# A two-layer mixture-of-experts kernel: first tiles by columns, one unit's gathers in a row, half blocks interleaved with whole ones

## The chip, the cores and the metric

The kernel runs on one core of a Trainium2 chip. The metric is the device time of one execution in microseconds (us): the median of three runs of the kernel before is 1027.73 us, the lowest 1024.75 and the highest 1029.03. TensorE (PE) multiplies matrices, VectorE (DVE), ScalarE (ACT) and GpSimd (POOL) do the rest, and SyncE (SP) and POOL issue most transfers.

## The reference

```python
x = windowed_attention(q, k, v, mem_k, mem_v)   # 4 x 8 heads x 768 x 64 -> 3072 tokens x 512
# layer 1: every token goes to one expert, each expert holds at most 3072 / 8 = 384 tokens
for e in range(8):
    mask = assigned == e                         # greedy, by falling logit
    out[mask] = np.maximum(x[mask] @ w1[e], 0) @ w2[e]      # 512 -> 1024 -> 512
x = out
# layer 2: every token goes to its two best experts by noisy logits, weighted by their softmax
for e in range(8):
    for k in range(2):
        mask = top2[:, k] == e
        out[mask] += top2_w[mask, k, None] * (np.maximum(x[mask] @ w1[e], 0) @ w2[e])
```

## The kernel before

After the attention (about the first tenth of the time) and the routing of the first expert come the eight experts of layer 1, one after the other, and then the eight of layer 2. An expert's tokens are fetched by indirect DMAs of POOL (gathers of 128 tokens into `xg`), transposed into `xT`, multiplied with the first weights into 8 tiles of the hidden layer (`mm1`, 12 matmuls each: 4 pieces of the 512 inputs, and 3 products of the high and low fp16 parts `w_jh`, `w_jl`), put through the relu, and multiplied with the second weights (`mm2`: 24 matmuls of 512 columns for each block of 128 tokens). The results of layer 2 (`z`, `pv`) are scattered into the output by POOL.

In layer 1 an expert has three blocks of 128 tokens. For k = 0 and k = 1 the gathered tokens are transposed by PE (8 transposes of 128x128 each into a PSUM tile `tps`, copied to `xT` by ACT), for later ones by a transposing DMA of SP.

In layer 2 an expert e has two units, numbered u = 2e and u = 2e + 1. The first holds blocks 0, 1 and 2 and, for e = 0 to 5, a half block (HALF = 3): 64 tokens for e = 0, 1, 2 (2 parts) and 32 for e = 3, 4, 5 (4 parts). The second holds blocks 4, 5 and 6. A half block is computed in 24 steps; a step splits the 512 output columns over its parts, so that 2 matmuls of 64x256 (4 of 32x128) stand side by side in PE's columns, on 64 (32) columns of weights each.

One main program issues PE's matmuls. Between them it calls `tick()`, which runs generators for all that lies beside: gathers, transposes, weight splits, routing, lists. A generator yields a planned time or a condition; a planner's cost of each instruction (`Pipe.account`) decides between which matmuls it is resumed. All instructions recorded so have line L68. Where the main program waits (`until`, `wait` with a `spare` tile), it issues matmuls on `ones` as filling. Every engine works its instructions off in the order in which they were issued. PSUM tiles come from pools: m1 has three buffers (tiles of `mm1`), m2 two (tiles of `mm2`, and `tps` before).

What the change touches: `split` (the weights' scaling), `mm1`, `mm2`, `transpose`, `gather1` (layer 1's gathers), `list2` (token lists of layer 2; a small matmul `dup` copies a half block's list, `lsh`, to the other partitions), `gathers2` (layer 2's gathers and transposes), `metas` (small DVE work on gathered tokens) and `moe1`, `moe2` (the main program). SP issues, in one queue, the transposing DMAs (`xT<-xg`) and the loads of the next weights (`st<-x_dram`).

Of the kernel before, what the change touches and what calls it, by code (L numbers as in the profile page):

```python
# [29 lines left out]
CAP = NTOK // E  # L30
# [1044 lines left out]
C_H = 1.0  # L1075

KF = 5
SLACKG = -200.0

METAS = 16000.0  # L1080
LATE = 6000.0
SLACKH = 500.0


def whole(i):
# [57 lines left out]
def split(ctx, i, st, eager):  # L1143
# [59 lines left out]
    def halves(j, s):  # L1203
        done = W["w1" if m == 0 else "w2"]
        n = order(i, j)
        yield lambda: ctx.wnext == n < len(ctx.wfree)
        ctx.wnext += 1
        hi, lo = (wp.tile([128, 1024], F16, tag=f"w{o}", name=f"w{i}_{j}{o}", bufs=12) for o in "hl")
        src = st[j]
        sj = s[:, j : j + 1]  # L1210
        yield max(pipe.t["s"] - 100, pipe.rdy("s", s))
# [24 lines left out]
    for j in range(4):  # L1236
        if i == 0 and j > 1:
            yield lambda: 0 in ctx.X1
# [30 lines left out]
    return ctx.m1.tile([128, DM], F32, tag="m1", name="m1")  # L1269


def mm1(ctx, k, xT, n, ps, last=True):

    pipe, W, hT = ctx.pipe, ctx.W[k], []
    for ft in range(FT):
        if ft:

            pipe.until(lambda: len(hT) > ft - 3)
            ps = tile1(ctx)
        if ft % 2 == 0:  # L1280
# [3 lines left out]
        ps = ps[:, :n]  # L1284
        fs = slice(128 * (ft % 2), 128 * (ft % 2) + 128)
        i = 0
        for kt in range(KT):
            for wo, xo in ((0, 0), (0, 1), (1, 0)):
                pipe.P.matmul(
                    ps, w1[wo][:, kt, fs], xT[:, KT * xo + kt, :n], start=(i == 0), stop=(i == 3 * KT - 1)  # L1290
                )
                i += 1
                if i < 3 * KT:
                    pipe.tick()
        h = ctx.hp.tile([128, 2, XN], F16, tag="hT", name="hT", bufs=FT + 1)
        if k < KF:
            h = h.rearrange("p o n -> p (o n)").bitcast(F32)[:, :n]
# [41 lines left out]
    return ps  # L1339


def mm2_f32(ctx, k, hT):

    pipe = ctx.pipe
# [13 lines left out]
    return ps  # L1358


def transpose(ctx, xT, rows, tile_):

    pipe = ctx.pipe
    yield pipe.rdy("p", tile_)
    ps = ctx.m2.tile([128, 2 * KT, 128], F16, tag="m2", name="tps")
    for kt in range(2 * KT):
        pipe.P.transpose(ps[:, kt], rows[:, 128 * kt : 128 * kt + 128], ctx.id16)
    pipe.S.activation(xT, ps, AF.Copy)


def gather1(ctx, k):

    pipe = ctx.pipe
    NA = CAP // 128
    xT = ctx.xp.tile([128, 2 * KT, XN], F16, tag="xT", name=f"xT{k}", bufs=3)
    ix = ctx.wk.tile([128, NA], F32, tag="ix1", name=f"ix1_{k}")
    xg = []
    yield pipe.rdy("g", ctx.idx1)
# [13 lines left out]
    for a in range(NA):  # L1392
        rows = xg[a][:, :DM].bitcast(F16)
        if k > 1:
            yield pipe.rdy("y", xg[a])
            pipe.D.dma_start_transpose(xT[:, :, 128 * a : 128 * a + 128], rows)
        else:
            yield from transpose(ctx, xT[:, :, 128 * a : 128 * a + 128], rows, xg[a])
# [120 lines left out]
def moe1(ctx):  # L1519
# [37 lines left out]
        pipe.add(g)  # L1557

    for k in range(E):
        ps = tile1(ctx)  # L1560
        if not k:
            pipe.until(lambda: 0 in ctx.gathered)
        pipe.until(lambda: k in ctx.X1 and k in ctx.W, ps)
        xT, ix = ctx.X1[k]
        hT = mm1(ctx, k, xT, CAP, ps)
        m1_done.add(k)
        ys = ctx.wk.tile([128, NA], F32, tag="ys", name=f"ys{k}")
        if k >= KF:
# [13 lines left out]
def list2(ctx, e, pi, wt, cols, late=0.0):  # L1582
# [12 lines left out]
    if HALF in cols:  # L1595
        h, m = cols.index(HALF), 128 // parts(e)
        sh = pool.tile([64, 3], F16, tag="lsh", name=f"lsh{e}")[:m]
        V_.tensor_copy(sh, six[:m, h])
        yield pipe.rdy("p", sh)
        pd = ctx.ms.tile([128, 3], F32, tag="mso", name=f"dup{e}")  # L1600
        P_.matmul(pd, ctx.dup[parts(e)][:m], sh, start=True, stop=True)
        V_.tensor_copy(six[:, h], pd)
# [88 lines left out]
def gathers2(ctx):  # L1691
    pipe, wk = ctx.pipe, ctx.wk
    V_ = pipe.V
    for e in range(E):
        for h, cols in enumerate(units(e)):
# [5 lines left out]
            xg = []  # L1701
            for a in cols:
                rows = ctx.rows2[e, a][0]
                yield max(pipe.rdy("g", rows), pipe.t["g"] - 100)
                g = ctx.xp.tile([128, ROW], F32, tag="xg", name=f"xg2_{e}_{a}", bufs=4)
                pipe.G.indirect_dma_start(
                    out=g, out_offset=None, in_=x2[:, :], in_offset=bass.IndirectOffsetOnAxis(ap=rows, axis=0)
# [2 lines left out]
            for a, g in zip(cols, xg):  # L1710
                m = 128 // parts(e) if a == HALF else 128
                s0 = 128 * (a - a0)
                yield pipe.rdy("y", g)
                pipe.D.dma_start_transpose(xT[:, :, s0 : s0 + m], g[:m, :DM].bitcast(F16))
            ctx.X2[u] = xT
# [4 lines left out]
def metas(ctx, e, u, cols, xg, meta):  # L1720
# [1 line left out]
    pipe, wk = ctx.pipe, ctx.wk  # L1722
    V_ = pipe.V
    na, a0 = len(cols), cols[0]
    yield pipe.rdy("v", *xg) + METAS * min(1.0, 0.5 * u)
    for a, g in zip(cols, xg):
        V_.tensor_copy(meta[:, a - a0], g[:, DM : DM + 2])
    tg = wk.tile([128, na], I32, tag="tg2", name=f"tg2_{u}", bufs=4)
# [40 lines left out]
def moe2(ctx):  # L1769
    pipe = ctx.pipe  # L1770
    for e in range(E):
        k = E + e
        for h, cols in enumerate(units(e)):
# [6 lines left out]
            ys = ctx.wk.tile([128, len(cols)], F32, tag="ys2", name=f"ys2_{u}")  # L1780
            pipe.V.tensor_scalar(ys, xw, ctx.W[k]["comb"], 1.0 / (C_H * WSC), op0=ALU.mult, op1=ALU.mult)
            pv = ctx.pv.pop(u, None)
            for c, a in enumerate(cols):
                ps = mm2(ctx, k, hT, 128 * c, parts(e) if a == HALF else 1, a == NA2 - 1)
                n = DM // parts(e) if a == HALF else DM
                if e:
                    z = pv[c]
# [130 lines left out]
def program(tc, t):  # L1918
# [3 lines left out]
    with (  # L1922
# [6 lines left out]
        with tc.manual_schedule(), tc.tile_pool(name="rt", bufs=1) as ctx.rt:  # L1929
            setup(ctx, cp)  # L1930
            attention(ctx)
            with (
# [12 lines left out]
                ctx.pipe.early.add(ctx.x2.tensor.name)  # L1945
                ctx.closed, ctx.sure, ctx.listed, ctx.est_known, ctx.gathered, ctx.spread = {}, {}, set(), set(), set(), 0
                ctx.st, ctx.split, ctx.W, ctx.wfree = {}, {}, {}, [0.0] * 12
                ctx.X1, ctx.Y, ctx.rowed, ctx.picked, ctx.gated = {}, {}, set(), 0, 0
                ctx.rows2, ctx.X2, ctx.M, ctx.pv, ctx.got2, ctx.u_done = {}, {}, {}, {}, set(), set()
                ctx.ovready = ctx.locked = ctx.ordered = False  # L1950
# [151 lines left out]
```

## Time and profile before

| | |
|---|---|
| median of three runs | 1027.73 us |
| profiled execution: device time | 1033.36 us |
| profiled execution: span | 1031.5 us |
| mean granted clock of PE | 0.983 |
| PE busy | 982.5 us, 95% of the span |
| DVE, ACT, POOL busy | 62%, 45%, 28% |

The span runs from the first instruction to the last; the device time is 1.9 us longer. PE is busy nearly all the time, so the order of PE's instructions is the order of the whole: time is gained where PE stands idle, or where it has less to do. What PE waited for is grouped in the view of waits; starts of single matmuls are in the timeline. The ends of matmuls are modelled, so the distance from one start to the next is the measure of what one takes.

### The profile page before, as it was taken

The page shows a single profiled execution, that of the slowest core. Times are in us where ns is not written, and L with a number is a line of the kernel's source. Part 1 is how long each engine was busy: PE and PEld are TensorE (multiplying, and loading weights), DVE is VectorE, ACT ScalarE, POOL GpSimd, SP SyncE. Part 2 cuts the span into 40 slices and gives each one's busy share as a digit, 9 for nine tenths or more (in the row PEclk, how much of TensorE's full clock was granted, in tenths as well). Part 3 has the DMA queues.
Part 4 walks back from the last instruction along what each step waited for, and adds up shares of the span by engine and source line. Part 5 has one row for each costly group of instructions (what it writes and reads, how often), then busy time and mean ns, then how long its engine had stood idle before and what let it go on. Part 6 is the DMA issues. An engine that isn't in the chain of part 4 may idle for free. (4 is left out here: it accounts for less than half of the span.)

```text
span 1031.5 us, 21798 instructions
## 1 busy us (share of the span) xinstructions
PE 982.5 (95%) x8278; PEld 589.7 (57%) x8278; DVE 639.0 (62%) x2095; ACT 466.7 (45%) x799; POOL 284.4 (28%) x468
## 2 busy tenths in 40 slices
PE   8989399999999999999989899999999999999997
PEld 5778377676767674554454454555544555555553
DVE  7988875676586776886757745457355454654221
ACT  6767153545262557977136445054260441523110
POOL 4765051010120312030223133133332332232221
PEclk9999599999999999999999999999999999999999
DMA  9998345575776759596188739367284591554410
GB/s 333 330 324 305 112 173 185 125 220 170 217 201 216 137 177 303 169 241 126 48 239 249 183 93 300 72 182 205 76 265 107 142 264 59 170 121 103 122 62 31
DMA packets 146848, 184.61 MB, mean 179 GB/s; under 512 B 105154, under 2 KB 105666, under 8 KB 145204
## 3 DMA queue, kind: packets, MB, share of 16 engines
q1 hardware_dynamic: 129410, 131.73, 44.7%
q0 software_dynamic: 13872, 45.15, 15.1%
q10 hardware_dynamic: 3458, 6.30, 1.7%
q8 instruction: 66, 1.08, 0.4%
q14 instruction: 42, 0.34, 0.1%
HBM read 127.10 MB, written 32.44 MB: 155 GB/s over the span
## 5 line engine op out<-in xcount | busy, mean ns | idle before, releaser
L68 PEld LDWEIGHTS <-hT 128*128 128x128 f16 (+2 forms) x1800 | 143.4, 98 | 163.3 <-issue 7.8
L68 ACT ACTIVATE hT<-m 128x384 f16<-128x384 f32 (+2 forms) x152 | 75.4, 499 | 282.2 <-PE m L68 258.3
L68 DVE SCALAR_TENSOR_TENSOR hT<-m,hT 128x384 f16<-128x384 f32 (+2 forms) x152 | 86.5, 570 | 105.6 <-ACT hT L68 91.2
L68 ACT ACTIVATE junk<-st 128x1024 f16<-128x1024 f32 x108 | 113.6, 1052 | 58.2 <-DMA st<-w_dram 30.2
L68 PE MATMUL m2f<-st,hT 128*128 128x256 f32 x480 | 127.6, 398 | 0.3 <-ACT hT L68 0.3
L68 POOL DMA_INDIRECT out_dram<-pv,ts x47 | 49.6, 1055 | 262.7 <-DVE pv L68 101.9
L68 DVE SCALAR_TENSOR_TENSOR pv<-m,ys,pv 128x512 f32<-128x512 f32 (+2 forms) x47 | 33.5, 714 | 117.4 <-PE m L68 117.3
L68 PE MATMUL m<-xT,w_0h 128*128 128x384 f16 (+2 forms) x384 | 97.9, 335 | 4.7 <-DMA xT<-xg 4.7
L68 PE MATMUL m<-xT,w_2h 128*128 128x384 f16 (+2 forms) x384 | 97.2, 333 | 1.7 <-DVE hT L68 1.7
L68 PE MATMUL m<-xT,w_3h 128*128 128x384 f16 (+2 forms) x384 | 97.1, 333 | 1.0 <-DVE hT L68 1.0
L68 PE MATMUL m<-xT,w_1h 128*128 128x384 f16 (+2 forms) x384 | 96.5, 331 | 0.0
L68 PEld LDWEIGHTS m2f<-st,hT 128*128 128x128 f32 x480 | 83.3, 190 | 10.0 <-ACT hT L68 0.7
L68 PE MATMUL m<-w_3h,hT 128*128 128x512 f16 (+2 forms) x300 | 71.7, 345 | 1.4 <-DVE hT L68 1.4
L68 PE MATMUL m<-w_2h,hT 128*128 128x512 f16 (+2 forms) x300 | 72.0, 345 | 0.9 <-issue 0.9
L68 PE MATMUL m<-w_0h,hT 128*128 128x512 f16 (+2 forms) x300 | 72.1, 346 | 0.0
L68 PE MATMUL m<-w_1h,hT 128*128 128x512 f16 (+2 forms) x300 | 71.5, 345 | 0.0
L68 PE MATMUL m<-xT,w_0l 128*128 128x384 f16 (+2 forms) x192 | 64.2, 335 | 0.0
L68 PE MATMUL m<-xT,w_2l 128*128 128x384 f16 (+2 forms) x192 | 64.0, 333 | 0.0
L68 PE MATMUL m<-xT,w_3l 128*128 128x384 f16 (+2 forms) x192 | 63.8, 332 | 0.0
L68 PE MATMUL m<-xT,w_1l 128*128 128x384 f16 (+2 forms) x192 | 63.5, 331 | 0.0
L68 POOL DMA_INDIRECT xg<-x,rows x54 | 54.2, 1004 | 29.5 <-issue 14.5
L68 POOL DMA_INDIRECT pv<-out_dram,tg x47 | 46.0, 979 | 51.7 <-DMA out_dram<-pv,ts 35.0
(350 smaller groups left out, 1827.4 us busy)
## 6 DMA issues: line engine op xcount, KB each, us to landing
st<-w_dram SPq DMA_DIRECT2D x64, 512.0 KB
st<-x_dram SPq DMA_DIRECT2D x64, 512.0 KB
v<-vctx_dram SPq DMA_DIRECT2D x24, 520.0 KB
k<-kT_dram SPq DMA_DIRECT2D x24, 312.0 KB
xr<-rb SPq DMA_DIRECT2D x24, 264.0 KB
x<-rb SPq DMA_DIRECT2D x24, 264.0 KB
q<-qT_dram SPq DMA_DIRECT2D x12, 512.0 KB
out_dram<-zero ACTq DMA_DIRECT2D x24, 256.0 KB
```

The lines of the kernel that those rows point to most:

```text
L68: return f(*args, **kw)
```

## The change

1. First expert (k = 0): a new function `first` computes the first two tiles of `mm1` by blocks of 128 columns, each as soon as its block of `xT` is copied, in 72 matmuls of 128 columns instead of 24 of 384. `xT` of k = 0 is stored block by block. Two of the weight splits wait for `X1` at another place.
2. Second expert (k = 1): its PE transposes are planned 3000 ns later (2 FAR1).
3. The matmul `dup` is planned 1500 ns later (FAR1).
4. Second unit of layer 2's first expert (u = 1): the gathers of blocks 4, 5 and 6 follow in a row, and block 6 is transposed by PE into an m1 buffer in place of a DMA. The eight transposes stand in PE's order inside unit 0's blocks 2 and HALF, behind the 16th matmul of block 2.
5. `metas` of unit 0 is planned 8000 ns later.
6. `mm2_both`: block 2 of a first unit and its half block are computed together. Nine matmuls of the whole block come first; then each further one is followed by one or two steps of the half block in turn.

```diff
+def first(ctx, tiles, spare):
+    pipe, W = ctx.pipe, ctx.W[0]
+    pipe.until(lambda: len(W["w1"]) > 0, spare)
+    w1 = W["w1"][0]
+    for a in range(CAP // 128):
+        pipe.until(lambda: len(ctx.part0) > a and ctx.part0[a][1] <= pipe.t["p"] + 60.0, spare)
+        pipe.wait(*w1, spare=spare)
+        xT = ctx.part0[a][0]
+        for ft, ps in enumerate(tiles):
+            i = 0
+            for kt in range(KT):
+                for wo, xo in ((0, 0), (0, 1), (1, 0)):
+                    pipe.P.matmul(
+                        ps[:, 128 * a : 128 * a + 128], w1[wo][:, kt, 128 * ft : 128 * ft + 128], xT[:, KT * xo + kt],
+                        start=(i == 0), stop=(i == 3 * KT - 1),
+                    )
...
+def mm2_both(ctx, k, hT, s0, s1, cut):
+    pipe, W = ctx.pipe, ctx.W[k]
+    m, n = 128 // cut, DM // cut
+    steps = [(ft, ho, wo) for ft in range(FT) for ho, wo in ((0, 0), (1, 0), (0, 1))]
+    whole_, split_ = (ctx.m2.tile([128, w], F32, tag="m2", name="m2") for w in (DM, n))
+    done = 0
+    for i, (ft, ho, wo) in enumerate(steps):
+        w2 = W["w2"][ft // 2]
+        pipe.P.matmul(
+            whole_, hT[ft][:, ho, s0 : s0 + 128], w2[wo][:, ft % 2], start=(i == 0), stop=(i == len(steps) - 1)
+        )
+        pipe.tick()
+        while done * (len(steps) - BEHIND) < (i + 1 - BEHIND) * len(steps):      # BEHIND = 8
+            ft, ho, wo = steps[done]
+            w2 = W["w2"][ft // 2]
+            for j in range(cut):
+                pipe.P.matmul(
+                    split_[m * j : m * j + m], hT[ft][:, ho, s1 : s1 + m], w2[wo][:, ft % 2, n * j : n * j + n],
+                    start=(done == 0), stop=(done == len(steps) - 1),
+                )
+            done += 1
+    return whole_, split_
...
-def transpose(ctx, xT, rows, tile_):
+def transpose(ctx, xT, rows, tile_, late=0.0, bank="m2"):
-    yield pipe.rdy("p", tile_)
-    ps = ctx.m2.tile([128, 2 * KT, 128], F16, tag="m2", name="tps")
+    yield pipe.rdy("p", tile_) + late
+    ps = getattr(ctx, bank).tile([128, 2 * KT, 128], F16, tag=bank, name="tps")
...
+        elif k:
+            yield from transpose(ctx, xT[:, :, 128 * a : 128 * a + 128], rows, xg[a], 2.0 * FAR1)
...
-        yield pipe.rdy("p", sh)
+        yield pipe.rdy("p", sh) + FAR1
         pd = ctx.ms.tile([128, 3], F32, tag="mso", name=f"dup{e}")
...
-                yield max(pipe.rdy("g", rows), pipe.t["g"] - 100)
+                yield max(pipe.rdy("g", rows), pipe.t["g"] - 100 if u != 1 else 0.0)
...
+                if u == 1 and a == cols[-1]:
+                    yield from transpose(ctx, xT[:, :, s0 : s0 + m], g[:m, :DM].bitcast(F16), g, FAR1, "m1")
+                    continue
...
-    yield pipe.rdy("v", *xg) + METAS * min(1.0, 0.5 * u)
+    yield pipe.rdy("v", *xg) + METAS * (1.0 if u > 1 else 0.5)
...
+                if HALF in cols and c == HALF - 1:
+                    both = mm2_both(ctx, k, hT, 128 * c, 128 * HALF, parts(e))
+                ps = both[a - HALF + 1] if both else mm2(ctx, k, hT, 128 * c, 1, a == NA2 - 1)
```

PE, layer 2, first expert, unit 0, before: the end of block 2 (`m2_8602`) and the start of the half block (`m2_8636`). An LDWEIGHTS loads the hidden tile `hT` that the next matmul uses, `w17_jh` and `w17_jl` are the second weights.

```order
L68 LDWEIGHTS hT_8453
L68 MATMUL m2_8602<-w17_3h_8233,hT_8453 128x512
L68 LDWEIGHTS hT_8453
L68 MATMUL m2_8602<-w17_3l_8234,hT_8453 128x512
L68 LDWEIGHTS hT_8265
L68 MATMUL m2_8636<-w17_0h_8156,hT_8265 64x256
```

The same place after, with block 2 as `m2_8635` and the half block as `m2_8636`; two steps (four matmuls) of the half block stand between the two whole ones.

```order
L68 LDWEIGHTS hT_8346
L68 MATMUL m2_8635<-w17_1l_8195,hT_8346 128x512
L68 LDWEIGHTS hT_8287
L68 MATMUL m2_8636<-w17_0h_8172,hT_8287 64x256
...
L68 LDWEIGHTS hT_8287
L68 MATMUL m2_8636<-w17_0h_8172,hT_8287 64x256
L68 LDWEIGHTS hT_8362
L68 MATMUL m2_8635<-w17_1h_8194,hT_8362 128x512
```

Before, PE goes once from whole to half matmuls and back to whole ones at the next `mm1`; after, it does so 16 times in this block.

POOL, layer 2, around the gathers of unit 1 (`xg_0_4` to `xg_0_6`), before; `out_dram<-z` are scatters of unit 0's results, block by block, the last one the half block's.

```order
L68 DMA out_dram<-z_8516,ts_0_8045 3072x512
L68 DMA xg_0_4_8586<-x_61,rows_0_8566 128x528
L68 DMA xg_0_5_8593<-x_61,rows_0_8566 128x528
L68 DMA out_dram<-z_8597,ts_0_8045 3072x512
L68 DMA xg_0_6_8606<-x_61,rows_0_8566 128x528
L68 DMA out_dram<-z_8631,ts_0_8045 3072x512
L68 DMA out_dram<-z_8741,ts_0_8045 6144x256
```

The same stretch after:

```order
L68 DMA out_dram<-z_8546,ts_0_8202 3072x512
L68 DMA xg_0_4_8619<-x_61,rows_0_8599 128x528
L68 DMA xg_0_5_8621<-x_61,rows_0_8599 128x528
L68 DMA xg_0_6_8623<-x_61,rows_0_8599 128x528
L68 DMA out_dram<-z_8630,ts_0_8202 3072x512
L68 DMA out_dram<-z_8782,ts_0_8202 3072x512
L68 DMA out_dram<-z_8787,ts_0_8202 6144x256
```

The scatter that stood between the gathers of blocks 5 and 6 now follows them.

PE, layer 1, first expert, before: the last filling matmul ahead of `mm1`, and `mm1`'s first three; `rps<-flf,onesb` is a step of the routing, whose input `flf` DVE writes.

```order
L68 MATMUL m_2538<-ones_67 128x128
L68 LDWEIGHTS w_0h
L68 MATMUL m_2538<-xT_2874,w_0h 128x384
L68 LDWEIGHTS w_0h
L68 MATMUL m_2538<-xT_2874,w_0h 128x384
L68 LDWEIGHTS w_0l
L68 MATMUL m_2538<-xT_2874,w_0l 128x384
L68 LDWEIGHTS onesb
L68 MATMUL rps_3113<-flf,onesb 128x8
```

The same place after, behind the routing's matmuls on `GE`:

```order
L68 LDWEIGHTS GE_2990
L68 MATMUL rps_3069<-OH_2982,GE_2990 15x8
L68 LDWEIGHTS w_0h
L68 MATMUL m_2903<-xT_2873,w_0h 128x128
L68 LDWEIGHTS onesb
L68 MATMUL rps_3107<-flf,onesb 128x8
L68 LDWEIGHTS w_0l
L68 MATMUL m_2903<-xT_2873,w_0l 128x128
```

Before, twelve filling matmuls and three of `mm1` stood between the matmuls on `GE` and the one on `flf`; after, one of 128 columns.

## Rows read from the trace of the kernel before

**Rows 1.** The page, section 1: busy time and share of each engine.

```profile
PE 982.5 (95%) x8278; PEld 589.7 (57%) x8278; DVE 639.0 (62%) x2095; ACT 466.7 (45%) x799; POOL 284.4 (28%) x468
```

**Rows 2.** Waits of PE: us in total, times, longest us.

```profile
PE m L68 <- DMA xT<-xg: 4.7, 1, 4.7
PE dup L68 <- DVE lsh L68: 3.4, 4, 2.1
PE tps L68 <- DMA xg<-xr,idx: 1.5, 2, 1.1
```

**Rows 3.** Timeline of PE, unit 0's end to unit 1's start: start, duration, instruction.

```profile
518.03 1.35 PE L68 MATMUL m<-ones 128*128 128x128 f16 x21
524.04 0.49 PE L68 MATMUL m<-xT,w_0h 128*128 128x384 f16 x2 [4.66 <-DMA xT<-xg]
```

**Rows 4.** Stretches: length, PE busy, granted clock, DMA share, GB/s.

```profile
524.00:527.00 3.00, 2.96 (x11) 0.58 0.93 287
527.00:530.00 3.00, 3.00 (x18) 0.85 1.00 395
```

**Rows 5.** Timeline of SP's queue around the same place.

```profile
512.43 2.86 SPq L68 DMA_TRANSPOSE xT<-xg  x2
...
518.26 2.42 SPq L68 DMA_TRANSPOSE xT<-xg  x1
...
521.77 4.26 SPq L68 DMA_DIRECT2D st<-x_dram  x8
```

**Rows 6.** Timeline of POOL: the gather of block 6.

```profile
513.53 0.97 POOL L68 DMA_INDIRECT xg<-x,rows  x1 [0.30 <-issue]
```

**Rows 7.** Timeline of PE: half block of 2 parts (expert 1).

```profile
594.91 0.59 PE L68 MATMUL m<-w_3h,hT 128*128 128x512 f16 x2
595.34 0.38 PE L68 MATMUL m<-w_3l,hT 128*128 128x512 f16 x1
595.65 0.41 PE L68 MATMUL m<-w_0h,hT 128*64 128x256 f16 x4
...
598.18 0.28 PE L68 MATMUL m<-w_3l,hT 128*64 128x256 f16 x2
598.39 0.50 PE L68 MATMUL m<-xT,w_0h 128*128 128x384 f16 x2
```

**Rows 8.** Timeline of PE: half blocks of 4 parts (experts 3, 4, 5).

```profile
732.02 0.30 PE L68 MATMUL m<-w_0h,hT 128*32 128x128 f16 x8
...
733.54 0.25 PE L68 MATMUL m<-w_3l,hT 128*32 128x128 f16 x4
733.73 0.50 PE L68 MATMUL m<-xT,w_0h 128*128 128x384 f16 x2
...
798.81 0.29 PE L68 MATMUL m<-w_0h,hT 128*32 128x128 f16 x8
...
799.10 0.23 PE L68 MATMUL m<-w_0l,hT 128*32 128x128 f16 x4
...
800.54 0.29 PE L68 MATMUL m<-w_2h,hT 128*32 128x128 f16 x6 [0.44 <-issue]
...
801.32 0.50 PE L68 MATMUL m<-xT,w_0h 128*128 128x384 f16 x2
...
865.63 0.30 PE L68 MATMUL m<-w_0h,hT 128*32 128x128 f16 x8
...
868.06 0.50 PE L68 MATMUL m<-xT,w_0h 128*128 128x384 f16 x2
```

**Rows 9.** Timeline of PE: first expert's start.

```profile
137.14 0.84 PE L68 MATMUL m<-ones 128*128 128x128 f16 x12
137.82 0.49 PE L68 MATMUL m<-xT,w_0h 128*128 128x384 f16 x2
...
143.02 0.49 PE L68 MATMUL m<-xT,w_1h 128*128 128x384 f16 x2
```

**Rows 10.** Timeline of DVE at that place.

```profile
137.79 0.15 DVE L68 TENSOR_TENSOR flf<-rps,capB 15x8 bf16<-15x8 f32 x1
```

More of the change, by code (lines that the diff above doesn't have):

```diff
@@ L1077 @@
 KF = 5
+FAR1 = 1500.0
 SLACKG = -200.0
@@ L1082 @@
 SLACKH = 500.0
+BEHIND = 8
 def whole(i):
@@ L1210, in halves @@
         sj = s[:, j : j + 1]
+        if i == 0 and j > 1:
+            yield lambda: 0 in ctx.X1
         yield max(pipe.t["s"] - 100, pipe.rdy("s", s))
@@ L1236, in split @@
     for j in range(4):
-        if i == 0 and j > 1:
-            yield lambda: 0 in ctx.X1
         yield lambda j=j: len(st) > j
@@ L1269, in tile1, with mm1 @@
     return ctx.m1.tile([128, DM], F32, tag="m1", name="m1")
-def mm1(ctx, k, xT, n, ps, last=True):
+def first(ctx, tiles, spare):
[14 more added lines that the diff above has]
+                    )
+                    i += 1
+                    if i < 3 * KT:
+                        pipe.tick()
+def mm1(ctx, k, xT, n, ps, last=True, done=()):
     pipe, W, hT = ctx.pipe, ctx.W[k], []
     for ft in range(FT):
-        if ft:
+        if ft and (ft != len(done) or not done):
             pipe.until(lambda: len(hT) > ft - 3)
-            ps = tile1(ctx)
-        if ft % 2 == 0:
+            ps = done[ft] if ft < len(done) else tile1(ctx)
+        elif done:
+            ps = done[ft] if ft < len(done) else ps
+        if ft % 2 == 0 and ft >= len(done):
             pipe.until(lambda: len(W["w1"]) > ft // 2, ps)
@@ L1283, in mm1 @@
             pipe.wait(*w1, xT, spare=ps)
-        ps = ps[:, :n]
         fs = slice(128 * (ft % 2), 128 * (ft % 2) + 128)
-        i = 0
-        for kt in range(KT):
+        i = 3 * KT if ft < len(done) else 0
+        out, spare = ps[:, :n], ps
+        if len(xT.shape) == 4:
+            out = out.rearrange("p (a n) -> p a n", n=128)
+        for kt in range(KT if not i else 0):
             for wo, xo in ((0, 0), (0, 1), (1, 0)):
+                x = xT[:, KT * xo + kt]
                 pipe.P.matmul(
-                    ps, w1[wo][:, kt, fs], xT[:, KT * xo + kt, :n], start=(i == 0), stop=(i == 3 * KT - 1)
+                    out, w1[wo][:, kt, fs], x if len(x.shape) == 3 else x[:, :n], start=(i == 0), stop=(i == 3 * KT - 1)
                 )
@@ L1294, in mm1 @@
                     pipe.tick()
+        ps = ps[:, :n]
         h = ctx.hp.tile([128, 2, XN], F16, tag="hT", name="hT", bufs=FT + 1)
@@ L1339, in mm2 @@
     return ps
+def mm2_both(ctx, k, hT, s0, s1, cut):
[9 more added lines that the diff above has]
+        )
+        pipe.tick()
+        while done * (len(steps) - BEHIND) < (i + 1 - BEHIND) * len(steps):
[8 more added lines that the diff above has]
+    return whole_, split_
 def mm2_f32(ctx, k, hT):
@@ L1375, in gather1 @@
     xT = ctx.xp.tile([128, 2 * KT, XN], F16, tag="xT", name=f"xT{k}", bufs=3)
+    if k == 0:
+        xT = xT.rearrange("p k n -> p (k n)")[:, : 2 * KT * CAP].rearrange("p (a k n) -> p a k n", a=NA, n=128)
     ix = ctx.wk.tile([128, NA], F32, tag="ix1", name=f"ix1_{k}")
@@ L1396, in gather1 @@
             pipe.D.dma_start_transpose(xT[:, :, 128 * a : 128 * a + 128], rows)
-        else:
-            yield from transpose(ctx, xT[:, :, 128 * a : 128 * a + 128], rows, xg[a])
+        elif k:
+            yield from transpose(ctx, xT[:, :, 128 * a : 128 * a + 128], rows, xg[a], 2.0 * FAR1)
+        else:
+            yield from transpose(ctx, xT[:, a], rows, xg[a])
+            ctx.part0.append((xT[:, a], pipe.rdy("p", xT)))
+    if k == 0:
+        xT = xT.rearrange("p a k n -> p k a n")
     ctx.X1[k] = (xT, ix)
@@ L1559, in moe1 @@
     for k in range(E):
+        done = ()
+        if not k:
+            pipe.until(lambda: 0 in ctx.gathered and 0 in ctx.W)
+            done = tile1(ctx), tile1(ctx)
         ps = tile1(ctx)
-        if not k:
-            pipe.until(lambda: 0 in ctx.gathered)
+        if done:
+            first(ctx, done, ps)
         pipe.until(lambda: k in ctx.X1 and k in ctx.W, ps)
         xT, ix = ctx.X1[k]
-        hT = mm1(ctx, k, xT, CAP, ps)
+        hT = mm1(ctx, k, xT, CAP, ps, done=done)
         m1_done.add(k)
@@ L1782, in moe2 @@
             pv = ctx.pv.pop(u, None)
+            both = ()
             for c, a in enumerate(cols):
-                ps = mm2(ctx, k, hT, 128 * c, parts(e) if a == HALF else 1, a == NA2 - 1)
+                if HALF in cols and c == HALF - 1:
+                    both = mm2_both(ctx, k, hT, 128 * c, 128 * HALF, parts(e))
+                ps = both[a - HALF + 1] if both else mm2(ctx, k, hT, 128 * c, 1, a == NA2 - 1)
                 n = DM // parts(e) if a == HALF else DM
@@ L1947, in program @@
                 ctx.st, ctx.split, ctx.W, ctx.wfree = {}, {}, {}, [0.0] * 12
+                ctx.part0 = []
                 ctx.X1, ctx.Y, ctx.rowed, ctx.picked, ctx.gated = {}, {}, set(), 0, 0
```

## The prediction

> **What bounds the kernel now.** I read the page's busy times first: PE is busy 95% of the span [rows 1], so no other engine bounds the kernel, and a change pays only where PE stood idle or did more than it must. The waits of PE come next [rows 2]. Three of them lie where the change works: 4.7 us once on the transposed tokens `xT`, 3.4 us over four `dup` matmuls (2.1 us in one of them), and 1.5 us over two waits of PE transposes on their gathers. The stretch of the largest wait is then read in the timeline and by its clock [rows 3, 4]: PE has nothing but filling from 518.03, the next `mm1` starts at 524.04, and the granted clock there is 0.58 and then 0.85, so PE runs at 1.2 GHz for part of it, after some 4.7 us without work. Last come the half blocks [rows 7, 8], where the distance between starts tells what a change of shape costs.
>
> All sums are made against the profiled execution (1033.36 us; its span of 1031.5 and 1.9 us around it) and moved to the median of the runs, 1027.73 us, which is 5.6 us lower: the difference of the two kernels is taken as the same.
>
> **The interleaved half blocks.** In a half block of 2 parts a whole matmul follows a whole one after 0.215 us (594.91, two of them, 595.34), the first half step follows the last whole one after 0.31, a step follows a step after 0.11 (595.65 to 598.18, 23 steps), and the next whole matmul follows the last step after 0.21 [rows 7]. So a change of shape costs about 0.095 us on the way in and 0.10 on the way out. Block 2 and half block together take now 23 x 0.215 + 0.31 + 2.53 + 0.21 = 8.0 us. After the change 8 whole matmuls are followed by a whole one, 16 by a half step, 8 half steps by a half step and 16 by a whole matmul: 8 x 0.215 + 16 x 0.31 + 8 x 0.11 + 16 x 0.21 = 10.9 us, or +2.9 us a block. The number of matmuls is the same; only the changes of shape grow from 2 to 32.
>
> With 4 parts a step takes 0.058 us (798.81 to 799.10, five steps), and the way out is 0.19 us from the last step's first matmul [rows 8]. I take 0.10 for the way out as with 2 parts, hence 0.16 in all; 0.13 (0.19 - 0.058) is the upper end. The three half blocks last 1.71, 2.51 and 2.43 us, against 23 x 0.058 + 0.16 = 1.5 without the idle time marked "issue" (0.44 us at one of its places). Eight instructions a step come too fast for PE's supply there; between whole matmuls that goes away. Block 2's own 23 x 0.215 + 0.31 = 5.26 us added, before is 6.97, 7.77 and 7.69 us; after is 8 x 0.215 + 16 x 0.31 + 8 x 0.058 + 16 x 0.16 = 9.7 us each, so +2.7, +1.9 and +2.0. The five half blocks of experts 1 to 5 together: 2 x 2.9 + 6.6 = +12.4 us, all of it on PE's path, with nothing to cover it. Expert 0's is in the next part. The trace has no alternating stream, so the bounds are wide: a switch that costs nothing in such a stream leaves -2.2 us (only the supply gaps go), the upper end of the way out makes +13.9.
>
> The Trainium skill speaks against this edit: in "TensorEngine Tiling (Array Packing)", section "Key Properties", it says that a change of tiling mode, and not merely of tile, drains TensorE. Rows 7 agree with it (0.095 and 0.10 us); by it every one of the 32 changes is paid, and the sum is the one above. The reading against it, that only the first matmul of a new output tile pays, would be the fast rival below.
>
> **The handover to unit 1.** PE's work on unit 0 ends at 518.03, `mm1` starts at 524.04 [rows 3]; the wait ends with the third transposing DMA, issued by SP from 518.26 to 520.68 and so in use 3.4 us after its issue ended [rows 5]. After the change two transposing DMAs are left. The second's issue ended at 515.29 (512.43 + 2.86), so by the same 3.4 us it is there at about 518.7. PE's own work ends at 518.03 + 2.9 (its interleaved half block) + 8 transposes x 0.057 (a 128-column matmul, twelve in 0.68 us [rows 9]) = 521.4. PE is then the later one, and `mm1` starts 2.6 us earlier than before. ACT's copy behind the transposes is hidden by the eight whole matmuls and their half steps that stand behind them. The idle time ahead of `mm1` goes, and with it the lower clock: 3 x (1 - 0.58) + 3 x (1 - 0.85) = 1.7 us [rows 4]. Together -4.3 us. There is a new wait in it: the transposes need block 6's gather. That was issued at 513.53 [rows 6] and its DMA transpose came 4.7 us later; it is issued about 1.8 us earlier now (the scatter between goes behind it), which makes 516.4 at the latest, where PE reaches the transposes at about 516.0 (the block starts 8.0 us ahead of 518.03; 16 whole matmuls and 11 steps take 8 x 0.215 + 7 x 0.31 + 4 x 0.11 + 7 x 0.21 + 0.2 = 6.0). Everything of unit 0 is queued behind them. I take 0.1 us for it: -4.2. If PE does not wait any less than before, the gain is 0.
>
> **The dup matmuls** stand 1.5 us later. Their four waits total 3.4 us [rows 2]; the longest, 2.1 us, loses 1.5, the three others (1.3 us in all) lose nearly all of theirs by the same 1.5: between -1.5 and -3.4, taken -2.6. Who waits for `dup` are the gathers of the next expert, tens of us ahead of their use. **The second expert's transposes** stand 3 us later, past the 1.1 us wait: -1.1, the tokens being used only in the next expert's `mm1`.
>
> **The first expert.** 72 matmuls x 0.057 = 4.1 us take the place of 24 x 0.162 (three times a 128-column matmul's columns, less its overhead) = 3.9. They may begin earlier: `mm1` begins at 137.82 behind twelve filling matmuls (0.68 us) [rows 9]. But PE's order now has the routing's matmul on `flf` behind the first narrow ones, and DVE writes `flf` from 137.79 to 137.94 [rows 10]: PE stops there, with the other 70 narrow matmuls queued behind, until about 138.0. The later tiles, from 143.02, come out at 0 either way; bounds -0.7 (all filling saved) and +0.6 (the wait, and the narrow matmuls' surplus). I take 0.
>
> The Trainium skill's "TensorE: Matmul & The Clock Gate", section "Back-to-back issue gap", gives some 81 ns for a matmul of 128 columns in a stream with weight loads. The row shows 57 ns in such a stream, so the measurement decides; by the page the narrow matmuls would take 5.8 us, and the forecast would be 1033.9.
>
> The later `metas` of unit 0 and the moved weight splits of expert 0 cost nothing: both stand ahead of uses that PE reaches only after 8 tiles of `mm1`, if DVE and ACT, at 62% and 45% [rows 1], keep their slack; uncovered, they would cost up to the 0.6 us already in the bounds.
>
> **Sum.** +12.4 - 4.2 - 2.6 - 1.1 + 0 = +4.5 us: 1037.9 us for the profiled execution, 1032.2 us for the median. 0.5%, about what a measurement of this kernel can tell from no change, is 5.1 us.
>
> **Rivals.** *Fast: an alternating stream does not pay for each change of shape.* For it: PE loads weights beside running matmuls, and the matmul that pays in rows 7 is also the first one of a new output tile. Against it: the way out is paid by the next `mm1` too, a quite different tile. The gross switch price in the five blocks is 12.4 + 2.2 = 14.6 us. At half of it the five blocks cost 5.1 us, the handover gains 1.5 more (-5.7), and the sum is -4.3: 1023.4 us. Free: -2.2 for the blocks, and `mm1` starts at 518.7 (-5.3 - 1.7), in all -12.9: 1014.8 us.
>
> *Slow: unit 1's tokens come no earlier.* Its one mechanism is the DMA queue at unit 1's start: eight weight loads, issued from 521.77 behind the third transpose [rows 5], are now issued right behind the second, some 5 us earlier, and the DMA engines are 93 to 100% busy there [rows 4]. If the second transpose's packets, or block 6's gather, are held up by them, `mm1` waits on. It decides from 521.4 on, where PE's own work ends; at the old 524.04, with the lower clock, the handover's -4.2 is lost: +8.7, 1036.4 us. For it speaks the fullness of the queue, against it that the loads stand behind the transposes in SP's order.
>
> *The waits only move:* `dup` and the transposes wait at their new places as long as before. That costs the gains of 2.6 and 1.1: 1035.9 us; the planned delays of 1.5 and 3 us against waits of at most 2.1 and 1.1 [rows 2] speak against it.
>
> **How the numbers follow.** The summed case has 0.66, with a range of its own of 1028 to 1036.5; the fast rival 0.15, the slow one 0.12, the moved waits 0.07. Faster by over 0.5% (under 1022.6) needs a switch at less than half price: 0.13. Slower by over 0.5% (above 1032.9) gets 0.25 of the summed case's 0.66 and the two slow rivals: 0.44. The rest, 0.43, is within. The range is 1020.5 to 1038.5: its lower end takes the half-price switch with some of the way to the free one, its upper end the slow rival with the way out at 0.13 us.
>
> **What would show it.** In the profile after: starts in the interleaved stretch 0.31 us from a whole matmul to a half one and 0.21 (0.16) us back, and 10.9 (9.7) us for such a pair of blocks; `mm1` of unit 1 starting right behind the last half step, with the granted clock at 1.00; the waits on `lsh` down to about 0.6 us and the one on the second expert's gather gone; the first expert's third tile within 0.7 us of 143.02. The forecast is wrong if a whole matmul follows a half one after no more than one step's time, or if `mm1` of unit 1 waits on `xT` again.

## The result, and the profile after

The changed kernel is slower: 1038.97 us in the median of five runs (1036.82 to 1044.55) against 1027.73 (1024.75 to 1029.03), a ratio of 1.0121 with a 95% interval of 1.0086 to 1.0156. The forecast was 1032.2 us, range 1020.5 to 1038.5. On another chip the two kernels came out at 1045.94 and 1031.48 us, again 1.0121.

PE's share of busy time has risen, from 95 to 96% and by 16.5 us; that is not more work done, since the matmuls are the same but for the eight transposes, the narrow ones and fewer fillings. From the page, section 1, of after:

```profile
PE 999.0 (96%) x8297; PEld 589.9 (57%) x8297; DVE 635.2 (61%) x2096; ACT 468.1 (45%) x800; POOL 285.6 (28%) x466
```

The waits of PE after (engine, line, released by: us in total, times, longest) have no `dup`, no `tps` and no `xT` left, where [rows 2] had 9.6 us of them. The first three below were there before as well (6.0, 3.4 and 4.1 us); the last is new, and small:

```profile
PE rps L68 <- DVE GE L68: 6.0, 5, 1.7
PE xb L355 <- DVE x L378: 4.2, 9, 1.1
PE m L68 <- DVE hT L68: 3.1, 2, 1.7
...
PE m L68 <- ACT hT L68: 0.7, 1, 0.7
```

So each wait that the change was to take away is gone in this execution. The interleaved blocks show where the time went. Timeline of PE after (start, duration, instruction; x4 is two steps of 2 parts), expert 1, then expert 3:

```profile
586.60 0.39 PE L68 MATMUL m<-w_1l,hT 128*128 128x512 f16 x1
586.92 0.30 PE L68 MATMUL m<-w_0l,hT 128*64 128x256 f16 x2
587.16 0.39 PE L68 MATMUL m<-w_2h,hT 128*128 128x512 f16 x1
587.48 0.41 PE L68 MATMUL m<-w_1h,hT 128*64 128x256 f16 x4
587.82 0.39 PE L68 MATMUL m<-w_2h,hT 128*128 128x512 f16 x1
...
727.60 0.39 PE L68 MATMUL m<-w_1h,hT 128*128 128x512 f16 x1
727.92 0.24 PE L68 MATMUL m<-w_0l,hT 128*32 128x128 f16 x4
728.09 0.39 PE L68 MATMUL m<-w_1h,hT 128*128 128x512 f16 x1
```

Read the starts: whole to half takes 0.32 us (586.60 to 586.92) and the way back 0.24 after a single step (586.92 to 587.16); two steps in a row take 0.34 with the way out (587.48 to 587.82). The 16 rounds of a pair of blocks, eight of each kind, are alike. A whole matmul after a whole one took 0.215 [rows 7]. With 4 parts it is 0.32 and 0.17. From the first matmul of block 2 to the next `mm1` expert 1's pair takes 11.45 us (582.99 to 594.44) against 8.04 (590.35 to 598.39); the five pairs of experts 1 to 5 together are 13.0 us longer.

The handover to unit 1, which answers to [rows 3, 4]: timeline of PE, then stretches (length, PE busy, granted clock, DMA share, GB/s).

```profile
515.98 0.61 PE L68 MATMUL tps<-id,xg 128*128 128x128 f16 x8
...
521.05 0.62 PE L68 MATMUL m<-w_3l,hT 128*128 128x512 f16 x3
521.60 0.50 PE L68 MATMUL m<-xT,w_0h 128*128 128x384 f16 x2
```

```profile
518.00:524.00 6.00, 6.00 (x41) 1.00 0.95 319
524.00:530.00 6.00, 6.00 (x59) 1.00 1.02 390
```

The transposes find their gather without a wait, `mm1` follows the last half step directly at 521.60 (forecast 521.4), and the clock stays at 2.4 GHz. In the first expert PE's stop before `flf` is there, short, and a wait on ACT follows that was not forecast; the third tile starts at 144.54 against 143.02 [rows 9], outside the 0.7 us that the forecast gave as a sign. At the next to last expert of layer 1 the difference is gone (`mm1` from 413.6, before 413.7). Timeline of PE after:

```profile
136.89 0.22 PE L68 MATMUL m<-xT,w_0h 128*128 128x128 f16 x1
...
138.21 0.23 PE L68 MATMUL m<-xT,w_0h 128*128 128x128 f16 x1
138.52 0.16 PE L68 MATMUL rps<-flf,onesb 15*128 15x8 bf16 x1
...
144.54 0.48 PE L68 MATMUL m<-xT,w_1h 128*128 128x384 f16 x2 [0.67 <-ACT hT L68]
```

The span of this profiled execution is 1037.1 us, 5.6 more than before's, close to the +4.5 of the sum. The medians are 11.2 us apart. So the open question was not only the interleaving, but why the two profiled executions stand closer than the medians.

### The profile page after: what moved, and what is told of

Its sections match the earlier page's. It is cut to its first block, busy times and chain, and to the rows that moved or that the text cites. A ratio compares the mean times of both kernels' runs of the same rounds, so it can differ in the third digit from the quotient of the medians.

```text
span 1037.1 us, 21841 instructions
## 1 busy us (share of the span) xinstructions
PE 999.0 (96%) x8297; PEld 589.9 (57%) x8297; DVE 635.2 (61%) x2096; ACT 468.1 (45%) x800; POOL 285.6 (28%) x466
## 5 line engine op out<-in xcount | busy, mean ns | idle before, releaser
L68 PE MATMUL m<-xT,w_0h 128*128 128x384 f16 (+3 forms) x416 | 97.3, 318 | 0.0
L68 PE MATMUL m<-w_2h,hT 128*128 128x512 f16 (+2 forms) x300 | 74.3, 348 | 0.0
L68 PE MATMUL m<-xT,w_0l 128*128 128x384 f16 (+3 forms) x208 | 65.2, 318 | 0.0
L68 POOL DMA_INDIRECT xg<-xr,idx x24 | 25.1, 1046 | 136.7 <-DVE idx L68 45.5
```

Of the source, the lines that this page charges most:

```text
L68: return f(*args, **kw)
```

## Experiments

All runs, with the kernel before timed beside them. The mean difference is that of all runs of a set to all runs of before in it, in us; its standard error, given in brackets in the text, is 0.7 to 1.6. The kernels between two lines ran on one chip, beside the same runs of before. Where an expectation names a time, it was set by the first median of before, 1027.7 us; on these chips before takes 1030 to 1033 us, so the ratios and the differences decide.

| kernel | runs | median | before | mean difference | ratio, 95% interval |
|---|---|---|---|---|---|
| before again | 10 | 1033.52 | 1033.02 | 0.0 | 0.9992, 0.9967 to 1.0017 |
| after, not interleaved | 12 | 1033.88 | 1033.02 | 0.0 | 1.0005, 0.9974 to 1.0035 |
| interleaving alone | 5 | 1043.76 | 1033.02 | +11.7 | 1.0103, 1.0069 to 1.0136 |
| after, 8 rounds | 10 | 1036.13 | 1033.02 | +3.1 | 1.0020, 0.9998 to 1.0042 |
| --- | | | | | |
| first expert alone | 12 | 1033.75 | 1032.27 | +1.3 | 1.0004, 0.9981 to 1.0028 |
| delays alone | 12 | 1028.87 | 1032.27 | -2.9 | 0.9967, 0.9950 to 0.9984 |
| unit 1 alone | 12 | 1028.58 | 1032.27 | -2.9 | 0.9970, 0.9946 to 0.9994 |
| not interleaved, again | 10 | 1029.46 | 1032.27 | -2.9 | 0.9966, 0.9944 to 0.9988 |
| --- | | | | | |
| after again | 6 | 1045.94 | 1031.48 | +13.9 | 1.0121, 1.0078 to 1.0165 |
| not interleaved, third | 12 | 1030.10 | 1031.48 | -1.7 | 0.9977, 0.9949 to 1.0005 |
| delays and unit 1 | 12 | 1027.55 | 1031.48 | -3.6 | 0.9960, 0.9935 to 0.9985 |
| first expert and delays | 12 | 1034.81 | 1031.48 | +2.9 | 1.0025, 0.9995 to 1.0056 |
| --- | | | | | |
| not interleaved, yT later | 12 | 1027.12 | 1030.27 | -3.5 | 0.9961, 0.9934 to 0.9988 |
| after, yT later | 10 | 1039.25 | 1030.27 | +8.6 | 1.0076, 1.0050 to 1.0101 |
| delays and unit 1, again | 12 | 1026.78 | 1030.27 | -4.3 | 0.9959, 0.9934 to 0.9984 |

**Before, unchanged.** No edit.

> The kernel before, unchanged, profiled and timed once more against itself. The forecast took the difference of two profiled executions and moved it to the median, although the profiled execution of before (1033.36 us) lay 5.6 us above that median, while that of the kernel after (1038.97 us) is its median. Theory P (the profiled execution of before was a long one of its kind): the time here is 1025 to 1029 us again, and a new profiled execution has a shorter span than 1031.5 us, by up to 5 us, lost at places that differ from run to run. Rival Q (a profiled execution of this kernel is always some 5 us longer): the new one takes 1032 to 1034 us again. Ratio 1.000 by both.

Its profiled span is 1031.6 us in a set whose runs of before reach from 1027.23 to 1039.26. So neither theory holds as put: on this chip the median itself is where the first profiled execution was. Executions of this kernel differ by several us, and so do the sets, each on its chip (medians of 1027.7 to 1033.0); a single pair of profiles says little below 5 us.

**Interleaving taken out, and put in alone.** Taken out of after, the call is as before the change:

```diff
-                if HALF in cols and c == HALF - 1:
-                    both = mm2_both(ctx, k, hT, 128 * c, 128 * HALF, parts(e))
-                ps = both[a - HALF + 1] if both else mm2(ctx, k, hT, 128 * c, 1, a == NA2 - 1)
+                ps = mm2(ctx, k, hT, 128 * c, parts(e) if a == HALF else 1, a == NA2 - 1)
```

> The kernel after with the half blocks behind block 2 again, as before the change; all its other parts stay. Theory S (every change of shape in the alternating stream is paid): 15 extra round trips in each of six blocks, 3.4 us a block of 2 parts and 3.1 to 3.9 of 4 parts before the supply gaps; those come back (2.2 us), so 16 to 18 us less than after, 1021 to 1023 us, and a ratio of 0.993 to 0.996 to before. Rival R (the loss against the median comes from the other parts: first expert, late transposes, unit 1): the time stays above 1030 us. Rival Q' (half of each): about 1027 to 1030 us.

> The kernel before with the interleaved half blocks as its only change. Theory S: six blocks pay, 3 x 3.4 for 2 parts and about 7 us for the 4-part blocks with their supply gaps gone, of which the first expert's 3.4 is covered by the wait on unit 1's tokens if that is as long as in the profiled execution: +13.5 to +17 us, 1041 to 1045 us, ratio 1.013 to 1.017. Rival R: the interleaving costs no more than 6 us of the loss: under 1034 us.

The interleaving alone costs 11.7 us (1.2), a little under theory S. On one chip after is 15.6 us (1.8) above itself without it, and the pair with `yT` later, below, stands 12.0 us (1.2) apart; the forecast's terms for this are 12.4 and, for expert 0's block, 2.9. But without the interleaving the kernel did not fall below before by the 4 to 7 us expected (10.7 by the forecast's own terms): 0.0 in this set, -2.9 and -1.7 in the two later ones. So the interleaving is shown to be the loss, and the gains of the rest are missing.

The profile of the interleaving alone shows one more thing. Its third transposing DMA and its gathers are as before the change, yet in this execution PE has no wait on `xT`: expert 0's longer block covers it. Timeline of PE, then a stretch:

```profile
521.77 0.62 PE L68 MATMUL m<-w_3l,hT 128*128 128x512 f16 x3
522.33 0.62 PE L68 MATMUL m<-ones 128*128 128x128 f16 x8
522.78 0.49 PE L68 MATMUL m<-xT,w_0h 128*128 128x384 f16 x2
```

```profile
518.00:524.00 6.00, 6.00 (x47) 1.00 0.66 165
```

Eight fillings (0.45 us) are all that is left of the 6 us of [rows 3], and the clock is at 1.00. From the start of layer 2's first `mm1` to that of its second expert's, this kernel takes 73.9 us (481.16 to 555.08), after 73.6 (479.99 to 553.62), before 77.4 (480.27 to 557.72). So beside the interleaving unit 1's edit had almost nothing left to gain.

**Half as many rounds.** `BEHIND = 16` for 8: the same matmuls, eight rounds of one whole matmul and three half steps.

> The kernel after with 17 whole matmuls ahead of the alternation instead of 9: eight rounds of one whole matmul and three half steps, so half as many changes of shape, and the same matmuls. Theory S: each block gives back 8 of its 15 extra round trips, some 8 x 0.22 = 1.8 us for 2 parts and 8 x 0.21 = 1.7 for 4 parts, less supply gaps that may come back: about 10 us less than after, 1028 to 1031 us. Rival F (a fixed cost of holding both blocks open, whatever the number of changes): no less than 1036 us.

Timeline of PE of this kernel, expert 1:

```profile
594.56 0.39 PE L68 MATMUL m<-w_2l,hT 128*128 128x512 f16 x1
594.88 0.41 PE L68 MATMUL m<-w_0h,hT 128*64 128x256 f16 x4
595.13 0.28 PE L68 MATMUL m<-w_0l,hT 128*64 128x256 f16 x2
595.33 0.39 PE L68 MATMUL m<-w_3h,hT 128*128 128x512 f16 x1
```

The price of a change is the same (0.32 in, 0.20 out), and the pair takes 9.63 us where after took 11.45 and before 8.04: 1.6 us for 7 extra rounds, 3.4 for 15. In blocks of 2 parts the loss goes with the number of changes, not with holding two blocks open. In blocks of 4 parts halving the changes won only 0.1 to 0.2 us a pair, for a reason given at the end. In time this kernel is 3.1 us above before, 9 to 11 less than after in its two sets (on other chips); theory S said about 10. It is as much above the kernel without interleaving on the same chip, where its five pairs (51.0 us against 43.5) lead one to expect 7.5; the spread of both (1026 to 1044 us) leaves that open.

**The other parts alone.** The first expert's tiles (after with `FAR1 = 0`, unit 1, `metas` and half blocks as before):

> The kernel before with the first expert's tiles by columns as its only change (the planned delays are set to 0, unit 1 and the half blocks as before). By the forecast's own step 0 us, -0.7 to +0.6: ratio 0.9993 to 1.0006. The profile of the kernel with all but the interleaving showed 0.85 us less at the first expert's second multiplication, yet its runs have the median of before and a wide spread (1026 to 1041 us). Theory V (this part makes the executions longer or more uneven, by stops of PE where there were filling matmuls, and so more time at the lower clock): 1.5 to 5 us slower than before in the median. Rival N (it does nothing to the median): within 1 us.

The planned delays:

```diff
+            yield from transpose(ctx, xT[:, :, 128 * a : 128 * a + 128], rows, xg[a], 2.0 * FAR1 if k else 0.0)
...
+        yield pipe.rdy("p", sh) + FAR1
```

> The kernel before with the two planned delays as its only change: the second expert's PE transposes 3 us later, the dup matmuls 1.5 us later. By the forecast -3.7 us (1.1 and 2.6): ratio 0.9964; its bounds are -1.5 and -4.5. If the other parts' gains are lost in the median because waits elsewhere take their place, it is 0 (1.000).

Unit 1 (gathers in a row, block 6 turned by PE, later `metas`), as in the change:

> The kernel before with unit 1's gathers in a row, its last block turned by PE and unit 0's later metas as its only change. PE's work on unit 0 ends 2.9 us earlier here than with the interleaved block, so the second transposing DMA decides (about 518.7 on the clock of the profile before): by the forecast's way -5.3 us of waiting and -1.7 of the lower clock, 7 us in all, ratio 0.993. Rival T (the tokens come no earlier in most executions): 0 to -1 us.

The first expert alone comes out at +1.3 us (1.1), which does not settle between its two theories. The delays give 2.9 us (0.7) of the 3.7 forecast. Unit 1 gives 2.9 (1.1) of 7. Its profile has new waits: on block 6's gather, and a few us later on DVE's `hT`, which comes later than PE now wants it. Timeline of PE with unit 1 alone:

```profile
516.54 0.62 PE L68 MATMUL tps<-id,xg 128*128 128x128 f16 x8 [0.57 <-DMA xg<-x,rows]
...
528.90 0.32 PE L68 MATMUL m<-xT,w_2h 128*128 128x384 f16 x1 [0.95 <-DVE hT L68]
```

And the wait that it takes away was longer in the profile of before than in others: 4.7 us there, and 3.3, 3.0, 3.9 and 3.6 in before again and in the three other profiles that have unit 1 and the half blocks as before. The lower clock is in four of these five (0.50 to 0.63 in the 3 us from `mm1`'s start, 1.00 in the kernel with first expert and delays). Taken over the stretch named above, to the second expert's `mm1`, the five take 74.5 to 77.4 us, before's the longest, and the seven profiles with unit 1's edit and no interleaving 71.7 to 72.8: 3.7 us less in the mean.

Unit 1's edit also takes most of the waits of `dup`, which it does not delay. Waits of PE with unit 1 alone, where [rows 2] has 3.4 us:

```profile
PE dup L68 <- DVE lsh L68: 0.8, 2, 0.5
```

**Without interleaving, again and a third time; after again.** The edits are those above.

> The kernel after without the interleaving, once more, for a second profile and more runs. Its profiled execution took 1025.6 us, 8 us less than that of before, while its runs have the median of before. Theory V (this kernel has long executions more often: stretches at the lower clock or a late transfer): a spread of 1026 to 1040 us again, mean 1033, and a longer profiled execution with the lost time at one or two places. Rival L (the first set of runs was unlucky): mean 1027 to 1029 us.

> The kernel after without the interleaving, for the comparison with after on the same chip and a third profile. Theory Y (with the first expert by columns and the delays together, the planner sets the routing's matmuls on yT five matmuls of mm1 earlier in the last expert of layer 1, where the transfer of yT is at times not there): a wait of PE on yT of up to 5 us in about half of the profiles, ratio 0.996 to 1.000. Rival A (the parts add up): ratio 0.992 to 0.994, 6 to 8 us.

> The kernel after, unchanged, once more, beside the same kernel without its interleaving on one chip. So far the interleaving alone made before 11.7 us slower in the mean (1.0103), and all the rest together came out 1.0005 and 0.9966. Theory S (32 paid changes of shape a block, a loss that the other parts don't give back): 8 to 12 us above before, ratio 1.008 to 1.012, and 10 to 13 us above the kernel without interleaving. Rival R (the 1.0121 of the first measurement was partly its chip): ratio 1.004 or less, as the profiled executions have it (5.6 us).

The second profile showed what no single part had shown: a wait of PE on `yT`, 3.2 us. `yT` is a block of layer 1's results, turned by a DMA of SP for layer 2's routing; PE's matmuls `lg` on it stand inside the last expert's `mm1`. After again has it too. Waits, timeline and stretches of PE, after again:

```profile
PE lg L68 <- DMA yT<-rb: 4.2, 1, 4.2
```

```profile
459.78 0.33 PE L68 MATMUL m<-xT,w_3h 128*128 128x384 f16 x1
464.30 0.40 PE L68 MATMUL lg<-wg2hl,yT 128*128 128x32 f16 x8 [4.20 <-DMA yT<-rb]
...
465.13 0.85 PE L68 MATMUL m<-xT,w_3h 128*128 128x384 f16 x2
```

```profile
464.40:471.00 6.60, 6.60 (x27) 0.55 1.19 259
```

After the wait PE runs at 1.2 GHz for most of 6.6 us (0.55), so that from the start of this `mm1` (444.31, before 447.68) to the start of layer 2's first (484.35, before 480.27) after again takes 7.5 us longer than before, and after in its first profile, without the wait, 0.4. Before, the same matmuls stand at `mm1`'s end and wait for nothing:

```profile
463.74 0.33 PE L68 MATMUL m<-xT,w_3l 128*128 128x384 f16 x1
463.91 0.35 PE L68 MATMUL lg<-wg2hl,yT 128*128 128x32 f16 x8
464.11 0.59 PE L68 MATMUL m<-w_0h,hT 128*128 128x512 f16 x2
```

SP's queue has the transfer: before, then after again (start, duration of the issue).

```profile
455.39 2.58 SPq L68 DMA_TRANSPOSE yT<-rb  x1
```

```profile
452.48 4.18 SPq L68 DMA_TRANSPOSE yT<-rb  x1
```

Before, PE comes to `yT` 5.9 us after the issue ended (457.97 to 463.91). After again it gets there at 460.1, 3.4 us after (456.66), and the block is usable only 7.6 us after. In the order of the instructions the matmuls on `yT` have moved from behind the 96th matmul of the last expert's `mm1` to behind the 91st. This order is that of every kernel here with both the first expert by columns and the delays, but for the two below that move these matmuls on purpose, and of no other. Of the seven profiles with it three had the wait (3.2, 4.6 and 4.2 us), of the eight of kernels without it none; chance alone makes such a split in one case of 13.

The earlier place is the smaller part of it. Counted from the start of this `mm1`, PE comes to `yT` 15.8 us on after again and 16.2 before. But the issue ends 12.3 us on where before it ended 10.3, and the block is usable 20.0 us on. In the order of before PE would have waited some 3.8 us for it too. The issue ends 10.3 to 12.3 us on in all nine profiles with the first expert and the delays, and 9.5 to 10.3 in the four that have the order of before. What makes the transfer late is not shown.

**Which parts bring it, and taking it out.**

> The kernel before with the first expert by columns and the planned delays: the smallest combination whose order has the matmuls on yT five matmuls earlier. The parts alone gave +1.3 and -3.0 us in the mean. Theory Y: the profile may show the wait on yT (3 to 5 us), mean within 1 us of before. Rival A: -2 to -3 us, ratio 0.997 to 0.998.

> The kernel before with the planned delays and unit 1's edit alone: neither the first expert by columns nor the interleaving. In its order the matmuls on yT stand no later than in the order of the delays alone. Theory Y: the two gains add up, -3.0 and -2.9 us in the mean, ratio 0.993 to 0.995, and no wait on yT. Rival A' (the two gains take the same idle time away): 0.996 to 0.997.

First expert and delays together, +1.3 and -2.9 alone, came out at +2.9 (1.3), above both bounds expected, though this one profile had no wait on `yT`. Delays and unit 1 gave -3.6 us, and -4.3 in a later set, where the two alone add up to -5.8: nearer to rival A', and in line with the waits of `dup` that unit 1 alone takes away, but within the errors not clear of the sum. Then the matmuls on `yT` were planned later and the rest of the two kernels kept:

```diff
-        yield pipe.rdy("p", yT[a]) + (2000 if k < E - 2 else 0)
+        yield pipe.rdy("p", yT[a]) + (2000 if k < E - 2 else 1000 if k == E - 2 else 0)
```

> The kernel after without the interleaving, and with the matmuls on yT of layer 1's last expert but one planned 1000 ns later, so that none stands between the 43rd and the 96th matmul of the last expert's mm1. Without that delay three sets of runs gave 0.05 us more, 2.9 and 1.7 us less than before in the mean. Theory Y: no wait on yT in the profile, mean 3.5 to 6 us below before, ratio 0.994 to 0.9965. Rival A' (the wait on yT is rare, the other gains are just smaller in most executions): mean 1 to 2.5 us below before.

> The kernel after, interleaving and all, with the same delay of the matmuls on yT. Theory Y: the loss of 12 to 14 us shrinks to about 9 to 11, ratio 1.0085 to 1.0105, no wait on yT. Rival A': 12 to 14 us again, ratio 1.012.

> The kernel before with the planned delays and unit 1's edit, the fastest so far (0.996, mean 3.6 us below before), once more on this chip for a firmer number: by the forecast's own sum of these parts 10.7 us, by the two parts measured alone 5.8 us, by the first measurement of both 3.6. Theory: 3.5 to 6 us below before, ratio 0.994 to 0.9965, no wait on yT.

After falls from +12.4 and +13.9 us in its two sets to +8.6, as theory Y had it, and its profile has no wait on `yT`. The kernel without interleaving gains 3.5 us (1.2) instead of 1.4 (0.7, the mean over its 34 runs): the expected direction, within the errors not more than that. The other sign of theory Y failed: its profile still has a wait on the moved matmuls, which now stand behind the first matmul of `mm2`:

```profile
463.35 0.36 PE L68 MATMUL lg<-wg2hl,yT 128*128 128x32 f16 x8 [1.92 <-DMA yT<-rb]
```

PE came there 16.8 us after `mm1`'s start (444.62), later than before, and the block was usable at 18.7. The stretch to layer 2 takes 36.6 us, 4.0 more than before. So PE waits for a late transfer even where these matmuls are planned later; planning them later shortens the wait only by what it moves them.

Among the fastest kernels is the one with delays and unit 1 alone: 0.9960 and 0.9959 in two sets, some 4 us under before, and clearly under after. The one without interleaving and with `yT` later is its equal within the errors (0.9961).

## Why the prediction was wrong

**The interleaving: right.** The forecast had 0.31 and 0.21 us for the way in and out, all 32 changes paid, and +12.4 us for experts 1 to 5; measured are 0.32, 0.20 to 0.24 and 13.0 us in the profile. As the only change it costs 11.7 us, net of the wait on `xT` that it covers. The fast rival (a stream that does not pay for each change) is out: every round in the trace pays, and with half the rounds a pair of 2 parts gives back 1.8 of its 3.4 us. The row that the sum went by held although it came from single changes. The Trainium skill, "TensorEngine Tiling (Array Packing)", section "Key Properties", has the rule that a change of tiling mode drains TensorE. Each of these rounds agrees with it, by the time lost; that a drain takes it the trace does not show.

**The step that failed: the gains set against it.** The sum booked -4.2, -2.6 and -1.1 for the handover, `dup` and the transposes, and 0 for the first expert: -7.9 us, or -10.7 where no interleaved block delays PE. The same edits without the interleaving gave -1.4 us (0.7). Three terms were mis-sized.

First, the 0 for the first expert. Alone its edit gives +1.3 us (1.1), but beside the delays and unit 1 it costs 2.5 (0.9; -1.4 against the -3.9 of both sets without it), and beside the delays alone 5.8 (1.5; +2.9 against -2.9, on two chips). The forecast looked at its tiles, up to the third, and for what waits behind `dup` only among the gathers. The loss that is seen lies some 320 us later, outside the places of the diff: with both edits PE comes to the matmuls on `yT` 0.4 to 0.6 us earlier and the transfer is later. Where PE waits, the last expert's stretch is 5 to 7.5 us longer than before, in three profiles of seven; that makes near 3 us an execution, if the seven are typical. With these matmuls later the mean fell by 3.9 and 5.4 us (after) and 2.1 (without interleaving), with errors of 1.4 to 1.9 and between chips. Why the transfer is late stays open, and so does whether the wait is the whole of the loss.

Second, the handover was priced from one execution, the longest of five. Unit 1 alone gained 2.9 us (1.1) in the runs and 3.7 in the profiles where 7 was the forecast. Of the missing 3.3, before's own profile accounts for 1.5 (77.4 us against the mean of 76.0); the rest is in line with the new waits of 0.6 and 0.95 us and the eight transposes. In after the stretch is 2.3 us under that mean, where 4.2 was booked, and 0.3 under the interleaving alone.

Third, the gains of `dup` and of the late transposes were right in mechanism, -2.9 us for -3.7 alone, but unit 1's edit takes part of the same waits, so that the two give -3.9 and not -5.8.

Together these are 1.9 us for the handover, 0.8 for the delays, 2.5 to 5.8 for the first expert and 0.6 for the interleaving: 5.8 to 9.1 of the 7.9 and 9.4 us by which the mean differences of after (12.4 and 13.9) lie above the sum.

That the pair of profiles agreed with the sum (+5.6 against +4.5) was luck. Before's profiled execution has the longest wait on `xT` of the five, and after's is one of those without the wait on `yT`. For the same reason the step "the difference of the two kernels is taken as the same" for profile and median could not hold: before's runs range over 12 us on one chip (1027.23 to 1039.26), and the profiled one (1033.36) lay above all five runs that after was first compared with.

**The rest.** The slow rival (unit 1's tokens no earlier) is out: `mm1` starts at 521.60, right behind PE's own work. That the waits only move is out for `dup` and `tps`; a new wait came at `yT`, which no rival had. The stated upper end of the range, the slow rival with the way out at 0.13 us, adds up to 1037.9 and not 1038.5.

## What to carry to other kernels

Changing the shape of PE's matmuls between full and part of the columns had a fixed price each way here, readable from one such place in the trace; group equal shapes, and alternate only if what is won is above about 0.2 us a round. Where a planner orders the program, compare the whole order and the transfers' times, not only the places of the diff: a wait far behind an edit can cost more than the edit brings. A wait that is to be removed should be read in several executions before its full length is booked, and it should be asked whether another part of the same change covers it anyway.

## What was not expected of the hardware

The way out of a half step is longer after a single step of 2 parts (0.23 to 0.24 us) than after two or three (0.20 to 0.21). It is the first step that takes longer, not the way out: before, the first two steps of expert 1's half block take 0.24 us (595.65 to 595.89), two later ones 0.22 (596.00 to 596.22). By the starts of single matmuls in both traces a first step takes 0.13 us and a later one 0.11, and the way out adds 0.10 in either case.

The gaps in PE's supply in half blocks of 4 parts (0.45 us, one to three a block) do not appear when one or two steps at a time stand between whole matmuls, but come back, at two or so a block, with three steps at a time: the 4-part pairs took 10.5 us with 8 rounds and 10.6 to 10.7 with 16, so halving the changes won next to nothing there. Waits of PE with 8 rounds; after has none in this group, before three:

```profile
PE m L68 <- issue: 2.7, 7, 0.5
```
